# A fused attention and mixture kernel: the second mixture's opening rebuilt, its weight operands asked for sooner, one tile moved

## The chip, the cores and the metric

The kernel runs on one core of one Trainium2 chip. The metric is the device time of one execution in microseconds, as the median over executions. Engines are called PE (TensorE), DVE (VectorE), ACT (ScalarE), POOL (GpSimd) and SP (SyncE, which here only starts transfers). Each engine works through its own instructions in order, and semaphores join them.

## The reference

Three stages follow one another, all in float32:

- Attention over 4 batches, 8 heads, 576 positions, head size 64: features exp(±(x·w_phi − max|x·w_phi|)), 256 of them, on q and k; then `num = q' (k'ᵀ v)`, `den = q' · sum(k')`, `out = num / den`. It gives x with 2304 rows and 512 columns.
- A first mixture: softmax over rows and over slots of `x @ phi` (32 slots, 4 for each of 8 experts); the slots' inputs go through each expert's `relu(s @ w1) @ w2` and are mixed back to rows.
- A second mixture, by far the longest: `P = exp(x @ w_gate − max)`, normalised eight times over rows and columns in turn, and `out = sum over 8 experts e of P[:, e] * (relu(x @ w1[e]) @ w2[e])`, with w1 512×1024 and w2 1024×512.

## The kernel before

In the second mixture the 2304 rows are taken in 9 blocks of 256 rows for each of 8 experts, 72 blocks in all, expert after expert. Rows of x have rank 32 there (they are mixtures of 32 slots), so the first layer is a product of slot weights `ct` (a transposed tile for every 512 rows, `ct0` to `ct4`) with a stack `st` made once for each expert (`make_stack`, `spread_stack`, done inside the expert's predecessor's last block).

The second layer is written as seven half-size products, k = 0 to 6, in the form of Strassen and Winograd. For each block, `hidden` makes seven left operands from the first layer's results z: a11, a12 and a22 are the relu of quarters of z, and s1 to s4 are sums and differences of them. For float32 accuracy every operand is split into a rounded high part (ACT, tiles `hh_a`, `hh_s`) and the rest (`hl_a` by DVE, `hl_s` by POOL), and each product is 12 matmuls of 128×128 by 128×256. The right operands come from w2: b11, b21, b22 as they are, t1 to t4 as sums and differences (`w_sum` 0 to 3, each one POOL instruction), and `w_part` k makes the high part (ACT) and the rest (POOL) of the operand of product k. Operands live in a ring of ten buffers (`n = (7 * e + k) % NW`), so part k of one expert takes the buffer of product k−3 of the expert before.

`hidden` is a generator of five steps. In the main loop the steps for block i+1 run behind products 2 to 6 of block i, one step behind each product. After product 2 of a block, `first_layer` computes z of the next block into two PSUM tiles, each of which exists once. Behind each product, `take` adds its sum into the output rows `xo` (ACT or DVE for expert 0, DVE with the factor P for the others).

Two dictionaries say behind which block and product the operands of the next expert are asked for: `W_SUMS` and `W_PARTS`, keys (block, k); a key (9, k) means block 0 of the expert itself. POOL does these and the `hl_s` of `hidden` in program order.

`sinkhorn` is the generator of P: gate product, gate pass `plog` (18 small matmuls), maximum, exponential, then eight rounds of five steps each on DVE with one small matmul. Its rounds are threaded through the blocks of expert 0: `SINK = {1: 3, 5: 2}` asks for three steps behind product 1 and two behind product 5.

From the end of the attention on, every engine keeps the order of the program (`InOrder`), so its instructions all carry line 50 in the profile; one goes by the tile names. Blocks are counted from 0 here, and k counts products. The opening is what stands between the first mixture's end and the main loop:

```
sink = sinkhorn(); next(sink)
stacks = {0: make_stack(0)}
for k in (4, 5, 6): w_part(0, k)
spread_stack(stacks[0], 0)
next(sink); next(sink)
first_layer(0, 0); first_layer(0, 1)
next(sink)
for _ in hidden(0): pass
load_munits(4)
```

Of the kernel before, what the change touches and what calls it, by code (L numbers as in the profile page):

```python
# [17 lines left out]
NT = NTOK // 128  # L18
# [35 lines left out]
def tile_kernel(ctx: ExitStack, tc: tile.TileContext, a):  # L54
# [48 lines left out]
    def load_k(t):  # L103
        x = kp.tile([128, 512], F32, tag="kt", name=f"kt{t}")
        SP.dma_start(out=x, in_=a["kT"][t])
        kt_t[t] = x
# [292 lines left out]
    load_k(1)  # L399
    load_v(0)  # L400
    load_k(2)
    ident = load_const("ident", [128, 128])
    ones = load_const("ones", [128, 128])
    sel_e = load_const("sel_e", [128, 4], kp)
# [113 lines left out]
    mp = mp_cm.__enter__()  # L518

    ct = [const.tile([128, 512], F32R, tag=f"x{i}", name=f"ct{i}", bufs=1) for i in range(4)]  # L520
    ct.append(const.tile([128, 256], F32R, name="ct4", bufs=1))
    rep = [const.tile([128, 4, 128], F32R, tag=f"x{4 + i}", name=f"rep{i}", bufs=1) for i in range(2)]
    for i in range(2):
        G.dma_start(out=rep[i], in_=a["rep"][:, i * 512:(i + 1) * 512].rearrange("p (g c) -> p g c", g=4))
# [201 lines left out]
    def acc_tile(name):  # L726
        return pm.tile([128, 512], F32, tag="m", name=name)
# [30 lines left out]
    def sinkhorn():  # L758

        pg = acc_tile("pgate")  # L760
        for c in range(KC):
            PE.matmul(pg[:, 0:E], sot[:, c, :], wg[:, c, :], start=c == 0, stop=c == KC - 1)
        gst = cp.tile([128, E], F32R, name="gst")
        V.tensor_copy(out=gst, in_=pg[:, 0:E])
        V.tensor_tensor(out=gst[64:128, :], in0=pg[64:128, 0:E], in1=gst[64:128, :].bitcast(F32), op=ALU.subtract)
        yield
        pl = acc_tile("plog")
        for t in range(NT):
            PE.matmul(pl[:, t * E:(t + 1) * E], ct[t // 4][:, t % 4 * 128:(t % 4 + 1) * 128], gst, start=True, stop=True)
        yield  # L770
        Pf = P.rearrange("p t e -> p (t e)")
        V.tensor_copy(out=Pf, in_=pl[:, 0:NT * E])
        gm = cp.tile([128, 1], F32, name="gm")
        V.tensor_reduce(out=gm, in_=Pf, axis=AX.X, op=ALU.max)
        yield
        pg = acc_tile("pgm")
        PE.transpose(pg[0:1, 0:128], gm, ident)
        gm1 = cp.tile([1, 1], F32, name="gm1")
        V.tensor_reduce(out=gm1, in_=pg[0:1, 0:128], axis=AX.X, op=ALU.max)
        pg = acc_tile("pgb")  # L780
        PE.matmul(pg[:, 0:1], ones[0:1, :], gm1, start=True, stop=True)
        yield
        V.tensor_copy(out=gm, in_=pg[:, 0:1])
        V.tensor_scalar_sub(Pf, Pf, gm)
        A.activation(out=P, in_=P, func=AF.Exp)
        yield
        for it in range(8):
            rs = cp.tile([128, NT, 1], F32, tag="rs", name=f"rs{it}")
            V.tensor_reduce(out=rs, in_=P, axis=AX.X, op=ALU.add)
            V.tensor_scalar_add(rs, rs, 1e-9)  # L790
            V.reciprocal(out=rs, in_=rs)
            yield
            V.tensor_tensor(out=P, in0=P, in1=rs.to_broadcast([128, NT, E]), op=ALU.mult)
            yield
            cs = cp.tile([128, 1, E], F32, tag="cs", name=f"cs{it}")
            csf = cs.rearrange("p o e -> p (o e)")
            V.tensor_reduce(out=csf, in_=P.rearrange("p t e -> p e t"), axis=AX.X, op=ALU.add)
            yield
            pg = z_tile(0, f"pcs{it}")
            PE.matmul(pg[:, 0:E], ones, csf, start=True, stop=True)  # L800
            V.tensor_scalar(out=csf, in0=pg[:, 0:E], scalar1=1e-9, scalar2=float(E) / NTOK, op0=ALU.add, op1=ALU.mult)
            V.reciprocal(out=csf, in_=csf)
            yield
            V.tensor_tensor(out=P, in0=P, in1=cs.to_broadcast([128, NT, E]), op=ALU.mult)
            yield
# [12 lines left out]
    def hidden(i):  # L818

        z0, z1 = zs.pop((i, 0)), zs.pop((i, 1))  # L820
        z11, z21 = z0[:, :, 0:128], z0[:, :, 128:256]
        z12, z22 = z1[:, :, 0:128], z1[:, :, 128:256]

        def raw(name):
            return cp.tile([128, KH, 128], F32, tag="s", name=f"{name}_{i}", bufs=3)

        def hi_of(name, src, func):
            h = cp.tile([128, KH, 128], F32R, tag="hh", name=f"hh_{name}_{i}", bufs=7)
            A.activation(out=h, in_=src, func=func)
            l = cp.tile([128, KH, 128], F32R, tag="hl", name=f"hl_{name}_{i}", bufs=7)  # L830
            hop[i, name] = h, l

        def lo_z(name, z):
            h, l = hop[i, name]
            V.scalar_tensor_tensor(out=l, in0=z, scalar=0.0, in1=h.bitcast(F32), op0=ALU.max, op1=ALU.subtract)

        def lo_s(name, s):
            h, l = hop[i, name]
            G.tensor_tensor(out=l, in0=s, in1=h.bitcast(F32), op=ALU.subtract)

        def fused(name, z, s, op):
            o = raw(name)
            V.scalar_tensor_tensor(out=o, in0=z, scalar=0.0, in1=s, op0=ALU.max, op1=op)
            return o

        r22 = raw("r22")
        if i:
            A.activation(out=r22, in_=z22, func=AF.Relu)
            hi_of("a11", z11, AF.Relu)
        else:  # L850
            hi_of("a11", z11, AF.Relu)
            A.activation(out=r22, in_=z22, func=AF.Relu)
            lo_z("a11", z11)
        s1 = fused("s1", z21, r22, ALU.add)
        yield
        s2 = fused("s2", z11, s1, ALU.subtract)
        hi_of("a12", z12, AF.Relu)
        hi_of("s1", s1, AF.Copy)
        lo_s("s1", s1)
        if i:  # L860
            lo_z("a11", z11)
        yield
        r11 = raw("r11")
        hi_of("s2", s2, AF.Copy)
        A.activation(out=r11, in_=z11, func=AF.Relu)
        lo_s("s2", s2)
        lo_z("a12", z12)
        s4 = fused("s4", z12, s2, ALU.add)
        yield
        hi_of("a22", z22, AF.Relu)  # L870
        hi_of("s4", s4, AF.Copy)
        s3 = fused("s3", z21, r11, ALU.subtract)
        lo_s("s4", s4)
        yield
        hi_of("s3", s3, AF.Copy)
        lo_z("a22", z22)
        lo_s("s3", s3)
        yield
# [43 lines left out]
    sink = sinkhorn()  # L922
    next(sink)
    stacks = {0: make_stack(0)}
    for k in (4, 5, 6):
        w_part(0, k)
    spread_stack(stacks[0], 0)
# [2 lines left out]
    first_layer(0, 0)  # L930
    first_layer(0, 1)
    next(sink)
    for _ in hidden(0):
        pass
    load_munits(4)

    W_SUMS = {(3, 1): 0, (3, 6): 1, (5, 6): 2, (7, 6): 3}
    W_PARTS = {(2, 6): 0, (4, 6): 2, (6, 6): 1, (8, 1): 3, (8, 6): 4, (9, 0): 5, (9, 1): 6}
    SINK = {1: 3, 5: 2}
    making = iter(())  # L940
    for i, (e, blk) in enumerate(blocks):
        more = e + 1 < E
        if blk == 2 and more:
# [1 line left out]
        for k in range(7):  # L945
# [15 lines left out]
            if e and (blk + 9, k) in W_PARTS:  # L961
                w_part(e, W_PARTS[blk + 9, k])
            if e == 0:
                for _ in range(SINK.get(k, 0) - (blk == 0 and k == 1)):
                    next(sink, None)
            if i == NBLK - 1 and k in (3, 4):
                scale_row(k - 3)
# [68 lines left out]
```

## Time and profile before

| | |
|---|---|
| median of 3 runs | 1088.23 us (1085.76 to 1088.39) |
| profiled execution | 1086.3 us, of which the span from first to last instruction is 1084.1 us |
| mean granted TensorE clock | 0.995 |
| busy shares of the span | PE 97%, PE weight load 91%, DVE 68%, POOL 63%, ACT 53% |
| chain that ended last | PE 78%, POOL 11%, DVE 5%, issue 2%, DMA 2%, ACT 1% |
| second mixture | from about 271 us to the end |

The shares are means over stages with different limits. The chain followed back from the last instruction says which engine's work set the end at each point: where POOL stands in it, PE was waiting for POOL or for what POOL released. In the timeline views a line gives the start of a group of instructions, how long it lasted, engine, line, operation, output and inputs, how many, and in brackets how long the engine stood idle before it and what ended that.

### The profile page before, as it was taken

How to read it: one execution, taken by the hardware profiler on the slowest of the kernel's cores; microseconds unless marked ns; L12 is line 12 of the kernel's file. 1: busy time of each engine (PE TensorE's matmuls, PEld its weight loads, DVE VectorE, ACT ScalarE, POOL GpSimd, SP SyncE). 2: the span in 40 equal slices, each digit the busy share in tenths (PEclk: the TensorE clock that was granted, in tenths of full speed). 3: DMA queues.
4: the chain of work that ended last, by engine and by line, in shares of the span. 5: the costliest groups of instructions: out<-in, count | busy, mean ns of one | idle time of the engine just before them, and what ended most of it. 6: DMA issues, size and time to landing. Idle time of an engine off the chain costs nothing.

```text
span 1084.1 us, 23152 instructions
## 1 busy us (share of the span) xinstructions
PE 1052.2 (97%) x9206; PEld 982.0 (91%) x9206; DVE 732.0 (68%) x1518; ACT 569.8 (53%) x1009; POOL 687.3 (63%) x442
## 2 busy tenths in 40 slices
PE   7999999999899999999999999999999999999998
PEld 5688788853899999999999999999999999999998
DVE  6878777850578767665766666576667666665765
ACT  5665544312556576654556454655555564545542
POOL 4776551107556777777777577767777775777443
PEclk9999999999899999999999999999999999999999
DMA  7772115379400130022003100300220031000111
GB/s 264 246 272 88 54 40 205 146 279 399 158 2 2 36 121 1 2 79 79 2 1 117 40 2 16 141 2 1 79 79 1 2 112 46 2 1 21 54 45 60
DMA packets 22571, 89.26 MB, mean 82 GB/s; under 512 B 2752, under 2 KB 5568, under 8 KB 14272
## 3 DMA queue, kind: packets, MB, share of 16 engines
q1 hardware_dynamic: 22176, 87.26, 22.2%
q8 instruction: 73, 1.20, 0.5%
q0 software_dynamic: 288, 0.52, 0.2%
q14 instruction: 34, 0.28, 0.1%
HBM read 83.05 MB, written 4.72 MB: 81 GB/s over the span
## 4 chain that ended last, share of the span: by engine, by line
PE 78%; POOL 11%; DVE 5%; issue 2%; DMA 2%; ACT 1%; SPq 0%; POOLq 0%; DVEq 0%; ACTq 0%
PE x L50 30%; PE y L50 14%; PE z L50 12%; PE num L271 6%; POOL hl_s L50 5%; POOL w_t L50 3%; PE kvacc L179 3%; POOL w_b L50 2%; PE ut L246 1%; PE ps L50 1%; DVE s L50 1%; PE kvp L218 1%; DMA moe_w<-in_moe_w 1%; PE pk L142 1%; PE ph L50 1%
## 5 line engine op out<-in xcount | busy, mean ns | idle before, releaser
L50 POOL TENSOR_TENSOR hl_s<-s,hh_s 128x512 fp32r<-128x512 f32 x288 | 367.5, 1298 | 230.1 <-ACT hh_s L50 214.0
L50 PE MATMUL x<-w_t,hh_s 128*128 128x256 f32 x1152 | 205.4, 278 | 3.9 <-DVE xo L50 2.7
L50 ACT ACTIVATE hh_s<-s 128x512 fp32r<-128x512 f32 x288 | 175.7, 629 | 53.0 <-DVE s L50 49.1
L50 PEld LDWEIGHTS x<-w_t,hh_s 128*128 128x128 f32 x1152 | 173.8, 188 | 5.3 <-issue 3.9
L50 DVE SCALAR_TENSOR_TENSOR xo<-x,P,xo 128x256 f32<-128x256 f32 x252 | 121.1, 481 | 75.3 <-PE x L50 75.3
L50 ACT ACTIVATE hh_a<-z 128x512 fp32r<-128x512 f32 x216 | 122.2, 600 | 90.1 <-DVE s L50 88.3
L50 ACT ACTIVATE r<-z 128x512 f32<-128x512 f32 x144 | 86.1, 598 | 156.6 <-PE z L50 156.2
L50 PE MATMUL x<-w_t,hl_s 128*128 128x256 f32 x576 | 159.7, 277 | 0.0
L50 DVE SCALAR_TENSOR_TENSOR s<-z,r 128x512 f32<-128x512 f32 x144 | 98.9, 687 | 86.7 <-ACT hh_a L50 82.2
L50 DVE SCALAR_TENSOR_TENSOR hl_a<-z,hh_a 128x512 fp32r<-128x512 f32 x216 | 147.4, 683 | 0.0
L50 DVE SCALAR_TENSOR_TENSOR s<-z,s 128x512 f32<-128x512 f32 x144 | 98.5, 684 | 19.4 <-POOL hl_s L50 17.9
L50 PE MATMUL x<-w_t,hh_a 128*128 128x256 f32 x576 | 104.2, 279 | 6.3 <-POOL w_t L50 4.9
L50 PEld LDWEIGHTS x<-w_t,hl_s 128*128 128x128 f32 x576 | 108.3, 188 | 0.0
L50 PE MATMUL y<-w_b,hh_s 128*128 128x256 f32 x576 | 103.8, 278 | 0.2 <-POOL w_b L50 0.2
L50 PE MATMUL x<-w_b,hh_a 128*128 128x256 f32 x576 | 103.1, 279 | 0.0
L50 PE MATMUL z<-w_b,hh_a 128*128 128x256 f32 x576 | 103.0, 279 | 0.0
L50 PE MATMUL y<-w_t,hh_s 128*128 128x256 f32 x576 | 102.9, 278 | 0.0
L50 PEld LDWEIGHTS x<-w_t,hh_a 128*128 128x128 f32 x576 | 87.5, 188 | 7.9 <-POOL w_t L50 6.2
L50 PEld LDWEIGHTS z<-w_b,hh_a 128*128 128x128 f32 x576 | 87.3, 189 | 2.9 <-issue 2.9
L50 PEld LDWEIGHTS y<-w_b,hh_s 128*128 128x128 f32 x576 | 87.5, 188 | 1.4 <-POOL w_b L50 1.3
L50 PEld LDWEIGHTS x<-w_b,hh_a 128*128 128x128 f32 x576 | 87.7, 190 | 0.0
L50 PEld LDWEIGHTS y<-w_t,hh_s 128*128 128x128 f32 x576 | 87.6, 188 | 0.0
(213 smaller groups left out, 2342.1 us busy)
## 6 DMA issues: line engine op xcount, KB each, us to landing
moe_w<-in_moe_w SPq DMA_DIRECT2D x64, 1024.0 KB, 6.9
vt<-in_vb SPq DMA_DIRECT2D x20, 256.0 KB, 3.7
kt<-in_kT SPq DMA_DIRECT2D x18, 256.0 KB, 3.1
qt<-in_qT SPq DMA_DIRECT2D x18, 256.0 KB, 2.8
out<-xo SPq DMA_DIRECT2D x18, 128.0 KB, 1.7
out<-xo SPq DMA_DIRECT2D x9, 256.0 KB, 2.0
rep<-in_rep POOLq DMA_DIRECT2D x2, 256.0 KB, 5.8
bd<-in_bd SPq DMA_DIRECT2D x1, 384.0 KB, 4.3
```

The source lines that it names most:

```text
L50: return lambda *args, **kwargs: self.tc.keep_in_program_order(make(*args, **kwargs))
L142: PE.matmul(o, hi[:, s], wbdh, start=True, stop=False)
L179: PE.matmul(acc[64 * j:64 * j + 64, p * 256:(p + 1) * 256], v[:, (2 * p + j) * D:(2 * p + j + 1) * D], phik[:, 2 * p + j].rearrange("p c f ...
L218: PE.matmul(ps[:, c * 192:(c + 1) * 192], kvt[:, p * 256 + c * 128:p * 256 + (c + 1) * 128], bd[:, p], start=True, stop=True)
L246: PE.transpose(ps[:, j * 128:(j + 1) * 128], uq_t[t][hh][:, j * 128:(j + 1) * 128], ident)
L271: PE.matmul(ps[r0:r1, j * XW:(j + 1) * XW], phiq[:, c, j * 128 + r0:j * 128 + r1], kvs_t[b][:, c, 4 * hh + j, :], start=c == 0, stop=c == 1,)
```

## The change

```
@@ attention's loads
     load_k(2)
+    ct4 = const.tile([128, 256], F32R, name="ct4", bufs=1)
     ident = load_const("ident", [128, 128])
@@ first mixture
-    ct.append(const.tile([128, 256], F32R, name="ct4", bufs=1))
+    ct.append(ct4)
@@ sinkhorn
         for t in range(NT):
             PE.matmul(pl[:, t * E:(t + 1) * E], ct[t // 4][...], gst, start=True, stop=True)
+            if t == NT // 2 - 1:
+                yield
         yield
@@
         V.tensor_reduce(out=gm1, in_=pg[0:1, 0:128], axis=AX.X, op=ALU.max)
+        yield
         pg = acc_tile("pgb")
@@ hidden
         hi_of("a12", z12, AF.Relu)
-        hi_of("s1", s1, AF.Copy)
-        lo_s("s1", s1)
         if i:
+            hi_of("s1", s1, AF.Copy)
+            lo_s("s1", s1)
             lo_z("a11", z11)
         yield
         r11 = raw("r11")
         hi_of("s2", s2, AF.Copy)
+        if i == 0:
+            hi_of("s1", s1, AF.Copy)
         A.activation(out=r11, in_=z11, func=AF.Relu)
         lo_s("s2", s2)
+        if i == 0:
+            lo_s("s1", s1)
         lo_z("a12", z12)
@@ the opening
     stacks = {0: make_stack(0)}
+    next(sink)
     for k in (4, 5, 6):
         w_part(0, k)
@@
-    for _ in hidden(0):
-        pass
+    making = hidden(0)
+    for _ in range(3):
+        next(making)
     load_munits(4)

-    W_SUMS = {(3, 1): 0, (3, 6): 1, (5, 6): 2, (7, 6): 3}
-    W_PARTS = {(2, 6): 0, (4, 6): 2, (6, 6): 1, (8, 1): 3, (8, 6): 4, (9, 0): 5, (9, 1): 6}
+    W_SUMS = {(3, 1): 0, (3, 6): 1, (5, 6): 2, (7, 1): 3}
+    W_PARTS = {(2, 6): 0, (4, 6): 2, (6, 6): 1, (8, 0): 3, (8, 1): 4, (8, 6): 5, (9, 0): 6}
     SINK = {1: 3, 5: 2}
-    making = iter(())
+    next_after = {(0, 0): 1}
@@ main loop
             if e == 0:
-                for _ in range(SINK.get(k, 0) - (blk == 0 and k == 1)):
+                for _ in range(next_after.get((blk, k), 0) + SINK.get(k, 0) - (blk == 0 and k == 1)):
                     next(sink, None)
```

In words. The tile `ct4` is allotted among the first constants instead of among the later ones. The gate pass is issued in two halves of 9 matmuls: the first between `make_stack` and `spread_stack`, the second where the whole stood. The broadcast of the maximum (`pgb`) moves from in front of block 0's products to behind product 0. For block 0 only three of the five steps of `hidden` come ahead of the loop, with the halves of s2 made before those of s1; the fourth and fifth step come behind products 0 and 1. For every next expert, sum 3 moves from behind product 6 to behind product 1 of block 7, part 3 from product 1 to product 0 of block 8, part 4 from product 6 to product 1 of block 8, part 5 from product 0 of the expert's own block 0 to product 6 of block 8, and part 6 from product 1 to product 0 of the expert's own block 0.

## Rows read from the trace of the kernel before

**Rows 1.** The list of waits (engine, line, waited for: us in total, times, longest).

```profile
PE x L50 <- POOL w_t L50: 4.9, 7, 0.7
```

**Rows 2.** PE timeline: first layers (start us, us), first handover, last handover.

```profile
391.25 1.11 PE L50 MATMUL z<-ct,st 128*128 128x256 f32 x8
...
403.56 1.11 PE L50 MATMUL z<-ct,st 128*128 128x256 f32 x8
...
978.23 1.11 PE L50 MATMUL z<-ct,st 128*128 128x256 f32 x8
...
988.71 1.10 PE L50 MATMUL z<-ct,st 128*128 128x256 f32 x8
...
1001.18 1.11 PE L50 MATMUL z<-ct,st 128*128 128x256 f32 x8
```

**Rows 3.** PE timeline: products late at the first handover.

```profile
394.93 0.53 PE L50 MATMUL y<-w_b,hh_s 128*128 128x256 f32 x2
...
397.42 0.39 PE L50 MATMUL x<-w_t,hh_a 128*128 128x256 f32 x1 [0.71 <-POOL w_t L50]
...
402.11 0.47 PE L50 MATMUL x<-w_t,hh_s 128*128 128x256 f32 x2 [0.45 <-DVE xo L50]
```

**Rows 4.** POOL timeline: experts 0 and 1, block 7 to the handover.

```profile
365.37 2.39 POOL L50 TENSOR_TENSOR w_b<-moe_w,w_b 128x1024 fp32r<-128x1024 f32 x1
...
376.20 2.39 POOL L50 TENSOR_TENSOR moe_w<-moe_w,t 128x1024 f32<-128x1024 f32 x1
...
380.54 2.40 POOL L50 TENSOR_TENSOR w_t<-moe_w,w_t 128x1024 fp32r<-128x1024 f32 x1 [1.95 <-ACT w_t L50]
...
390.25 2.41 POOL L50 TENSOR_TENSOR w_t<-moe_w,w_t 128x1024 fp32r<-128x1024 f32 x1
...
392.61 2.41 POOL L50 TENSOR_TENSOR w_b<-moe_w,w_b 128x1024 fp32r<-128x1024 f32 x1
...
394.98 2.39 POOL L50 TENSOR_TENSOR w_t<-moe_w,w_t 128x1024 fp32r<-128x1024 f32 x1
...
397.32 2.54 POOL L50 TENSOR_TENSOR hl_s<-s,hh_s 128x512 fp32r<-128x512 f32 x2
```

**Rows 5.** POOL timeline: expert 1, block 7.

```profile
469.81 2.54 POOL L50 TENSOR_TENSOR hl_s<-s,hh_s 128x512 fp32r<-128x512 f32 x2 [1.85 <-ACT hh_s L50]
```

**Rows 6.** DVE timeline: a take while POOL makes a part.

```profile
391.45 0.48 DVE L50 SCALAR_TENSOR_TENSOR xo<-x,P,xo 128x256 f32<-128x256 f32 x1 [0.88 <-PE x L50]
```

**Rows 7.** POOL timeline: expert 0, block 3, sum 0.

```profile
323.12 2.40 POOL L50 TENSOR_TENSOR moe_w<-moe_w 128x1024 f32<-128x1024 f32 x1
```

**Rows 8.** DVE timeline: expert 0, rounds on P, block 3 and block 7.

```profile
320.95 2.25 DVE L50 TENSOR_TENSOR P<-P,cs 128x144 f32<-128x144 f32 x1
...
323.58 1.97 DVE L50 TENSOR_SCALAR rs<-rs 128x18 f32<-128x18 f32 x1
...
368.30 0.18 DVE L50 TENSOR_SCALAR rs<-rs 128x18 f32<-128x18 f32 x1
```

**Rows 9.** PE timeline: expert 0, block 3, product 6.

```profile
328.18 0.50 PE L50 MATMUL x<-w_t,hh_a 128*128 128x256 f32 x2 [1.42 <-DVE xo L50]
```

**Rows 10.** PE timeline: the opening.

```profile
277.06 1.19 PE L50 MATMUL pr<-st,rep 128*128 128x256 f32 x8 [1.06 <-issue]
...
287.78 0.39 PE L50 MATMUL x<-w_t,hh_s 128*128 128x256 f32 x1 [1.16 <-ACT xo L50]
...
289.27 1.11 PE L50 MATMUL z<-ct,st 128*128 128x256 f32 x8
```

**Rows 11.** DVE timeline: the opening, s4 and the rest of a22.

```profile
284.87 0.69 DVE L50 SCALAR_TENSOR_TENSOR s<-z,s 128x512 f32<-128x512 f32 x1 [0.73 <-POOL hl_s L50]
...
286.72 0.68 DVE L50 SCALAR_TENSOR_TENSOR hl_a<-z,hh_a 128x512 fp32r<-128x512 f32 x1
```

**Rows 12.** Stretches (us; busy PE, PEld, DVE, ACT, POOL; clock; DMA): opening's low clock.

```profile
282.80:283.60 0.80, 0.80 (x6) 0.80 (x5) 0.77 (x3) 0.66 (x2) 0.04 (x1) 0.50 0.98 358
...
284.40:285.20 0.80, 0.80 (x5) 0.80 (x5) 0.33 (x1) 0.29 (x1) 0.80 (x2) 0.50 0.99 399
```

More of the change, by code (lines that the diff above doesn't have):

```diff
@@ L401, in tile_kernel @@
     load_k(2)
+    ct4 = const.tile([128, 256], F32R, name="ct4", bufs=1)
     ident = load_const("ident", [128, 128])
@@ L520, in tile_kernel @@
     ct = [const.tile([128, 512], F32R, tag=f"x{i}", name=f"ct{i}", bufs=1) for i in range(4)]
-    ct.append(const.tile([128, 256], F32R, name="ct4", bufs=1))
+    ct.append(ct4)
     rep = [const.tile([128, 4, 128], F32R, tag=f"x{4 + i}", name=f"rep{i}", bufs=1) for i in range(2)]
@@ L769, in sinkhorn @@
             PE.matmul(pl[:, t * E:(t + 1) * E], ct[t // 4][:, t % 4 * 128:(t % 4 + 1) * 128], gst, start=True, stop=True)
+            if t == NT // 2 - 1:
+                yield
         yield
@@ L779, in sinkhorn @@
         V.tensor_reduce(out=gm1, in_=pg[0:1, 0:128], axis=AX.X, op=ALU.max)
+        yield
         pg = acc_tile("pgb")
@@ L857, in hidden @@
         hi_of("a12", z12, AF.Relu)
-        hi_of("s1", s1, AF.Copy)
-        lo_s("s1", s1)
         if i:
+            hi_of("s1", s1, AF.Copy)
+            lo_s("s1", s1)
             lo_z("a11", z11)
@@ L864, in hidden @@
         hi_of("s2", s2, AF.Copy)
+        if i == 0:
+            hi_of("s1", s1, AF.Copy)
         A.activation(out=r11, in_=z11, func=AF.Relu)
         lo_s("s2", s2)
+        if i == 0:
+            lo_s("s1", s1)
         lo_z("a12", z12)
@@ L924, in tile_kernel @@
     stacks = {0: make_stack(0)}
+    next(sink)
     for k in (4, 5, 6):
@@ L932, in tile_kernel @@
     next(sink)
-    for _ in hidden(0):
-        pass
+    making = hidden(0)
+    for _ in range(3):
+        next(making)
     load_munits(4)
-    W_SUMS = {(3, 1): 0, (3, 6): 1, (5, 6): 2, (7, 6): 3}
-    W_PARTS = {(2, 6): 0, (4, 6): 2, (6, 6): 1, (8, 1): 3, (8, 6): 4, (9, 0): 5, (9, 1): 6}
+    W_SUMS = {(3, 1): 0, (3, 6): 1, (5, 6): 2, (7, 1): 3}
+    W_PARTS = {(2, 6): 0, (4, 6): 2, (6, 6): 1, (8, 0): 3, (8, 1): 4, (8, 6): 5, (9, 0): 6}
     SINK = {1: 3, 5: 2}
-    making = iter(())
+    next_after = {(0, 0): 1}
     for i, (e, blk) in enumerate(blocks):
@@ L963, in tile_kernel @@
             if e == 0:
-                for _ in range(SINK.get(k, 0) - (blk == 0 and k == 1)):
+                for _ in range(next_after.get((blk, k), 0) + SINK.get(k, 0) - (blk == 0 and k == 1)):
                     next(sink, None)
```

## The prediction

> **What bounds the kernel now.** I read the page's busy shares and its chain of waits first, then the list of waits, then the timelines of PE, POOL, ACT and DVE around each place that the change touches. The reader is to see that PE is the bound nearly everywhere in the second mixture, so only PE's idle time and its low clock can be won there. The first layers mark the blocks: from 978.23 to 988.71 us one block takes 10.48 us, and at that pace PE has no gaps [rows 2]. The list of waits names one thing that holds PE seven times, a part of the right operands made by POOL: 4.9 us in all [rows 1]. Seven is the number of handovers from one expert to the next. Each handover costs more than that entry shows: between the first layers on its two sides lie 391.25 to 403.56, or 12.31 us, at the first, and 988.71 to 1001.18, or 12.47 us, at the last [rows 2]. The losses over 10.48 us are 1.83 and 1.99 us; added over the seven handovers they are 13.9 us.
>
> Why the first handover loses its 1.83 us is seen in three PE lines: product 5 starts with a pair that lasts 0.53 us, product 6 waits 0.71 us for POOL, and product 2 of the next block waits 0.45 us for DVE's take [rows 3]. POOL's lines show one cause for all three. From 390.25 to 397.37 us POOL makes parts 4, 5 and 6 in one piece, and only then the two subtractions for s1 and s2 [rows 4]. Part 5 ends at 395.02 and part 6 at 397.37 us, just when PE needs them. The subtractions come late too, so DVE, which needs a buffer that the first of them frees, runs its takes late.
>
> **The change part by part.**
>
> *Parts 3 to 6 asked for sooner.* No instruction is added; four POOL and four ACT instructions move for each of seven experts. POOL's order becomes: part 3 in the time after 376.2, part 4 where part 3 stood (380.54), part 5 where part 4 stood (390.25), part 6 where part 5 stood (392.61 to 395.02) [rows 4]. Part 3 finds POOL free because sum 3, which ran at 376.20, leaves that place. Part 5 is then ready 2.27 us before product 5's line at 394.93, part 6 about 1.3 us before product 6 would start, and the subtractions start at about 395.0 instead of 397.32. They would like to start some 0.3 us before that, at the pace of other blocks; DVE stands idle 0.88 us between takes [rows 6], so this is covered. The ring doesn't hold the parts back: part k needs the product k−3 of the expert before, and each is asked for behind that product. The gain is therefore up to 13.9 us; if the backlog only moved it would be 0. I take 13.9, as POOL's free times before 380.54 (1.95 us idle even with sum 3 there [rows 4]) hold one more instruction of 2.4 us. If that cover were gone, each handover would keep its 1.8 to 2.0 us.
>
> *Sum 3 behind product 1 of block 7.* Seven POOL instructions of 2.39 us move ahead of that block's subtractions. In experts 1 to 6 POOL stands idle 1.85 us there [rows 5], so the subtractions come 0.5 us late; DVE's 0.88 us between takes [rows 6] cover it: nothing, with 7 × 0.5 = 3.5 us as the far end. In expert 0 it is not nothing. There POOL makes part 1 at 365.37 [rows 4] and sum 3 would follow at once, until about 370.1, while DVE does the rounds on P. Block 3 has just that sequence now, a part and then a sum at 323.12 [rows 7]: DVE's product on P lasts 2.25 us and ends with POOL's part, the addition on `rs` lasts 1.97 us and ends with POOL's sum, where the same addition takes 0.18 us in block 7 [rows 8]. PE then waits 1.42 us for DVE at product 6 [rows 9]. I charge block 7 of expert 0 the same, 1.4 us; between 0 and 2.4 us, the whole of sum 3.
>
> Here a page bears on the case. The Trainium skill, "SBUF — State Buffer", section "SBUF: two separate sides", says that VectorE and GpSimd share one pair of ports as an exclusive lock for a whole instruction, when VectorE's has two inputs in SBUF or runs in a two-port mode; the loser waits. Rows 8 agree for the operations on P, and by that rule the 1.4 us must be paid; were bandwidth merely shared, the sum below would be 1.4 us better. The same rule leaves alone an operation that reads PSUM, and the take of 0.48 us beside a part of POOL [rows 6] agrees.
>
> *The opening.* Before, PE waits 1.06 us ahead of `spread_stack` for DVE's stack and 1.16 us ahead of product 2 for the take of product 0, which stands on ACT behind all of `hidden` [rows 10]; and the clock is at 0.50, the level of 1.2 GHz, in the three stretches of 0.8 us from 282.8 to 285.2 us, under products 0 and 1 (the first and the last in [rows 12]). Nine matmuls of the gate pass now fill the 1.06 us, so z, and all that follows, comes about 1.0 us sooner. With two steps of `hidden` behind products, the take gets its place early and product 2 starts without its wait. But the two subtractions on POOL change places: s4, which waits for the one of s1 and starts at 284.87 now [rows 11], waits for the second of the pair instead: 1.0 sooner and, with POOL's second subtraction ahead (1.27 us, half of the pair in [rows 5]) and ACT's hi part of s2 starting behind s2 instead of s1 (0.7), 2.0 later, so at about 285.9. Behind it on DVE come s3, the take of product 1 and the rest of a22. That last one is at 286.72 now [rows 11] and would be at about 287.45, ending at 288.1. The next first layer overwrites the tile that it reads, and so can't start before 288.2; it starts at 289.27 now [rows 10]. The gain is 1.1 us at that point, and PE stands idle in front of it for 1 to 2 us. Two things can take it back: the subtraction on P, waiting for POOL's last two subtractions as in rows 8, makes the next block's `hidden` late; and idle PE time could bring the low clock back a few us later, as the sparse stretch ahead of 282.8 did. Bounds: at best all of 1.06 + 1.16 and half of the 2.4 us at low clock, 3.4 us gained; at worst POOL's 1.27 and a low stretch of its own, 1.2, so 2.5 us lost. I take 0.4 us gained, the 1.1 less what a chance of about a half of either loss is worth. The broadcast `pgb` behind product 0 costs nothing: its result is wanted only behind product 1.
>
> *`ct4` moved, SP and POOL's other queues.* The tile keeps its size and nothing else lies in its place: 0, and neither engine nor queue waits more. The four loads of the opening (SP) issue nothing new and no transfer is moved past them; part 6's earlier end lets the next loads start about 2 us sooner, and nothing waits for those in the list of waits: 0.
>
> The sum is −13.9 + 1.4 − 0.4 = −12.9 us. Made against the profiled execution's 1086.3 us (span 1084.1 and 2.2 us around it), it gives 1073.4; against the median of the runs, 1088.23, it gives 1075.3. I say **1075 us**. By itself this case reaches from 1071 (opening at its best) to 1079 (opening at its worst, 0.4 us late in each block 7).
>
> **The rivals.**
>
> *Half of the handover stays.* Parts 5 and 6 come in time but the subtractions still come late enough that product 2 waits for the take. For it: part 6 still stands in front of them and ends at about 395.0, a little after they could start. Against: DVE's 0.88 us idle. It would save 0.14 + 0.71 us of the first handover's lines [rows 3], about 6 us in seven; with the other terms, 6.0 − 1.4 + 0.4 = 5.0 us: about 1083.
>
> *The parts come no sooner.* The program asks sooner, but ACT's casts stand in order behind others and behind the product that frees the buffer, so POOL runs the same train. For it: at 380.54 POOL's wait ended with ACT's cast, which stands behind the stack's casts [rows 4]. Against: part 3 now stands ahead of those. Then only the 1.4 us and the opening remain: about 1089, within what counts as no change.
>
> *Slower: POOL's moved instructions hold DVE everywhere.* The rule of rows 8 would hold for DVE's reads of PSUM as well. Sum 3 would cost what block 3 pays, 1.42 us [rows 9], in all seven blocks 7, and part 3, which now runs while DVE casts the stack in block 8, would put `spread_stack` back by up to 2.4 − 0.5 = 1.9 us. Seven times 3.3 is 23.2 us, less 13.9: 9.3 us slower, about 1097. It decides from 2.0 us for each expert. Against it: rows 6.
>
> **How the numbers follow.** The forecast gets 0.74, half a handover 0.14, no sooner 0.07, slower 0.05. The range of 8 in 10 runs from 1070 to 1083, from a little under the forecast's own lower end to the half handover. A measurement of this kernel tells from no change what is over about 0.3%, 3.3 us. The first two cases are faster but for a small part: 0.87. The third is no change, with a little of the second: 0.07. The rest, 0.06, is slower.
>
> **What would show it.** In the profile after: the list of waits has no line of PE waiting for `w_t` from POOL seven times; the first layers at the handovers are 10.5 us apart; POOL's two subtractions follow part 6 at about the time of rows 4's 394.98, shifted by what was won before. In block 7 of expert 0 the addition on `rs` lasts about 2 us and product 6 has a new wait of some 1.4 us for DVE's take. In the opening the wait of 1.06 us is gone, the first layer of block 1 waits for DVE, and a second low stretch of the clock either comes behind it or doesn't. Wrong would be handovers of over 11 us, or blocks 7 of experts 1 to 6 longer than now.

## The result, and the profile after

The changed kernel takes 1071.2 us, the median of 4 runs (1068.3 to 1076.1), against 1087.1 us for the kernel before in the same series (1085.8 to 1088.4). The ratio is 0.986 [0.982, 0.990], so some 15 us are gone (11 to 20). The forecast was 1075 us.

The profiled execution after has a span of 1066.3 us, 17.8 us less than before. The list of waits of TensorE is read first (the tile that PE was to write, the engine and tile that it waited for; total us, times, longest us). The rows left out here are the attention's, and some of under 1 us:

```profile
...
PE x L50 <- DVE xo L50: 2.8, 2, 1.4
...
PE z L50 <- DVE gm L50: 2.3, 1, 2.3
...
```

The entry that stood seven times before, PE waiting for `w_t` from POOL [rows 1], is gone. The largest that are left in the second mixture are two waits for `xo`, 1.4 us each, of which the one in block 3 of expert 0 stood there before [rows 9], and one for `gm`, 2.3 us. The first layers stand so (PE timeline of after, around the first handover and the last):

```profile
378.39 1.11 PE L50 MATMUL z<-ct,st 128*128 128x256 f32 x8
...
388.87 1.11 PE L50 MATMUL z<-ct,st 128*128 128x256 f32 x8
...
399.35 1.11 PE L50 MATMUL z<-ct,st 128*128 128x256 f32 x8
...
973.43 1.11 PE L50 MATMUL z<-ct,st 128*128 128x256 f32 x8
...
983.91 1.11 PE L50 MATMUL z<-ct,st 128*128 128x256 f32 x8
```

Both handovers, 388.87 to 399.35 and 973.43 to 983.91, now take 10.48 us, where 12.31 and 12.47 stood [rows 2]; so do the five between them. POOL shows why (its timeline of after, where rows 4 showed the train):

```profile
373.99 2.39 POOL L50 TENSOR_TENSOR w_t<-moe_w,w_t 128x1024 fp32r<-128x1024 f32 x1
378.16 2.40 POOL L50 TENSOR_TENSOR w_t<-moe_w,w_t 128x1024 fp32r<-128x1024 f32 x1 [1.77 <-ACT w_t L50]
...
387.87 2.41 POOL L50 TENSOR_TENSOR w_b<-moe_w,w_b 128x1024 fp32r<-128x1024 f32 x1
390.23 2.41 POOL L50 TENSOR_TENSOR w_t<-moe_w,w_t 128x1024 fp32r<-128x1024 f32 x1
392.60 2.55 POOL L50 TENSOR_TENSOR hl_s<-s,hh_s 128x512 fp32r<-128x512 f32 x2
```

Parts 3 and 4 now stand at 373.99 and 378.16. At the end of the preparation POOL makes two parts (5 and 6) in one piece, not three, and the subtractions follow at 3.7 us behind the first layer at 388.87; before, they came 6.1 us behind theirs (397.32 against 391.25, [rows 2, 4]).

The whole difference of the two profiled executions adds up over four stretches of PE's timeline. "z" is the first first layer of the second mixture, at 280.00 before and 275.67 after.

| stretch | before, us | after, us | difference |
|---|---|---|---|
| start to the gate's first product | 271.46 | 269.75 | −1.71 |
| gate's first product to z | 8.54 | 5.92 | −2.62 |
| z to the end of the last matmul | 800.73 | 787.22 | −13.51 |
| behind the last matmul | 3.37 | 3.37 | 0.00 |

The first row and 1.6 us of the second are not the change's: before, the granted clock was 0.57 from 159 to 163 us and 0.50 (1.2 GHz) from 272 to 275 us, after it was 1.00 in these places. The run times, which have such stretches on either side, show 2 us less than the profiles do.

The third row is the change. The seven handovers give 13.88 us. The interval that ends expert 0 (first layer of block 8 to the next one, with the late products of block 7 and the next stack in it) grew from 14.44 to 15.91 us, 1.47 us. The opening from z to the first layer of block 2 grew from 20.03 to 20.56, 0.53 us. A part that I had not forecast falls on the same interval of the other experts, 13.74 to 13.54 us, six times 0.20, and on the last block, 16.67 to 16.10. That is −13.88 + 1.47 + 0.53 − 1.20 − 0.57 = −13.65, against −13.51; most of what is missing is one interval of expert 6, 10.57 us before and 10.76 after.

### The profile page after: what moved, and what is told of

Same layout as the page of the kernel before. It is cut to its first block, busy times and chain, and to the rows that moved or that the text cites. A ratio compares the mean times of both kernels' runs of the same rounds, so it can differ in the third digit from the quotient of the medians.

```text
span 1066.3 us, 23151 instructions
## 1 busy us (share of the span) xinstructions
PE 1039.9 (98%) x9206; PEld 974.1 (91%) x9206; DVE 734.3 (69%) x1518; ACT 571.5 (54%) x1009; POOL 688.3 (65%) x442
## 4 chain that ended last, share of the span: by engine, by line
PE 90%; DVE 4%; POOL 2%; issue 2%; DMA 2%; ACT 1%; SPq 0%; DVEq 0%; POOLq 0%; ACTq 0%
PE x L50 36%; PE y L50 18%; PE z L50 15%; PE num L271 6%; PE kvacc L179 2%; PE ut L246 1%; PE ps L50 1%; PE kvp L218 1%; DMA moe_w<-in_moe_w 1%; PE ph L50 1%; PE pk L142 1%; PE pk L144 1%; POOL zs L197 1%; PE pq L142 1%; PE pq L144 1%
## 5 line engine op out<-in xcount | busy, mean ns | idle before, releaser
L50 PE MATMUL x<-w_t,hh_a 128*128 128x256 f32 x576 | 101.9, 277 | 2.8 <-DVE xo L50 2.8
L50 PE MATMUL y<-w_b,hh_s 128*128 128x256 f32 x576 | 101.5, 276 | 0.0
```

The lines of the kernel that those rows point to most:

```text
L50: return lambda *args, **kwargs: self.tc.keep_in_program_order(make(*args, **kwargs))
```

## The experiments

"Block n's interval" is the time from the first layer that computes z of block n to the next one; the handovers are block 1's intervals of experts 1 to 7. The kernel before was run beside each of them; its median was 1086.4 us for the first eight, 1087.6 us for the last four. A difference in us is the ratio's distance from 1 times that median.

**The handover dictionaries alone.** The kernel before, with

```
-    W_SUMS = {(3, 1): 0, (3, 6): 1, (5, 6): 2, (7, 6): 3}
-    W_PARTS = {(2, 6): 0, (4, 6): 2, (6, 6): 1, (8, 1): 3, (8, 6): 4, (9, 0): 5, (9, 1): 6}
+    W_SUMS = {(3, 1): 0, (3, 6): 1, (5, 6): 2, (7, 1): 3}
+    W_PARTS = {(2, 6): 0, (4, 6): 2, (6, 6): 1, (8, 0): 3, (8, 1): 4, (8, 6): 5, (9, 0): 6}
```

> The kernel before with the two dictionaries alone changed (sum 3, parts 3 to 6 asked for sooner), opening and ct4 as before. Theory (POOL's train of parts at the handover is the loss): the first layers at all seven handovers are 10.5 us apart instead of 12.3 to 12.6, block 7 of expert 0 is 1.4 us longer, and the time is 12.5 us below before. Rival (the opening, or ct4's place, carries much of the change's gain): the time is under 8 us below before. Rival (parts come no sooner): 0 to 1.4 us slower.

Measured: 1076.0 us, ratio 0.989 [0.988, 0.991], 11.5 us less (9.6 to 13.4). All seven handovers take 10.48 us, and in expert 0 PE waits once more for the take behind DVE's rounds (PE timeline):

```profile
372.60 0.50 PE L50 MATMUL x<-w_t,hh_a 128*128 128x256 f32 x2 [1.25 <-DVE xo L50]
```

Its interval from z to the end of the last matmul is 788.31 us, 12.42 less than before: 13.88 less 1.47. So the handover is the dictionaries' alone, and most of the gain; the rival of under 8 us is out.

**Everything but the dictionaries.** The kernel after with the two lines of before.

> The changed kernel with the two dictionaries as before: only opening and ct4 are new. Theory: handovers 12.3 to 12.6 us apart as before; block 0's first layer about 1 us sooner after the gate product than before at equal clock, block 1's first layer waits some 2.2 us for DVE, and by block 2's first layer 0.4 us are left: the time is 0 to 0.5 us below before, plus or minus what low stretches of the clock make. Rival (opening worth 4 us, the 4.2 us by which block 1's first layer is earlier in the profile after): 3 to 4 us below before in every pair of profiles with the same mean clock.

Measured: 1084.7 us, ratio 0.999 [0.997, 1.000], 1.4 us less (0 to 2.8). The handovers are back at 12.3 to 12.6 us; the interval of block 8 stays at 13.54 us. The rival's 3 to 4 us are out. The two experiments make up the change: 11.5 and 1.4 us are 12.9, inside the 11 to 20 of the whole.

**Sum 3 back behind product 6.** The kernel after, with

```
-    W_SUMS = {(3, 1): 0, (3, 6): 1, (5, 6): 2, (7, 1): 3}
+    W_SUMS = {(3, 1): 0, (3, 6): 1, (5, 6): 2, (7, 6): 3}
```

> The changed kernel with sum 3 behind product 6 of block 7 again, parts 3 to 6 as changed. Theory (POOL's two instructions in one piece beside the rounds on P cost 1.4 us in block 7 of expert 0, and POOL has room before the handover): block 7 of expert 0 back to its 14.4 us between first layers, handovers still 10.5 us; 1.4 us below the changed kernel. Rival (part 3 needs the place of sum 3, so the train at the handover comes back): handovers of 11 to 12.5 us, 4 to 12 us slower than the changed kernel.

Measured: 1070.8 us, ratio 0.985 [0.983, 0.987]. The last interval of expert 0 is 14.24 us (365.92 to 380.16), where after has 15.91: the step costs 1.67 us, and the wait of 1.39 us in it is gone. The seven handovers stay at 10.48 us, so sum 3's move was not needed for them. The time is only 0.4 us under that of after, within the scatter of either. The profiled execution shows what runs of this kernel differ by: a stretch at half clock right where the prediction feared one (busy time by engine of three stretches, then the granted clock):

```profile
283.80:287.80 4.00, 1.76 (x15) 1.59 (x14) 3.08 (x6) 1.63 (x3) 2.05 (x3) 1.00 0.56 233
288.00:291.60 3.60, 3.60 (x21) 3.60 (x20) 2.94 (x6) 1.82 (x6) 1.01 (x1) 0.55 0.02 5
292.00:296.00 4.00, 4.00 (x37) 4.00 (x37) 2.74 (x6) 2.81 (x7) 2.55 (x2) 1.00 0.00 0
```

PE is busy 1.76 of the 4 us around its wait for the first layer of block 1 (at 287.14), and behind that the clock is at 0.55 with PE busy throughout. Block 1's interval is then 12.44 us in place of 11.15.

**One GpSimd step a block.** The kernel after, with

```
-    W_SUMS = {(3, 1): 0, (3, 6): 1, (5, 6): 2, (7, 1): 3}
-    W_PARTS = {(2, 6): 0, (4, 6): 2, (6, 6): 1, (8, 0): 3, (8, 1): 4, (8, 6): 5, (9, 0): 6}
+    W_SUMS = {(2, 6): 0, (3, 6): 1, (5, 6): 2, (7, 6): 3}
+    W_PARTS = {(1, 6): 0, (4, 6): 2, (6, 6): 1, (8, 0): 3, (8, 1): 4, (8, 6): 5, (9, 0): 6}
-        if blk == 2 and more:
+        if blk == 1 and more:
```

> The changed kernel with one sum or part behind product 6 of each of the blocks 1 to 7 (part 0, sum 0, sum 1, part 2, sum 2, part 1, sum 3) and parts 3 to 6 as changed, so that no two POOL instructions on weights stand in one piece beside the rounds on P. Theory (the lock on the port holds DVE's addition on rs until the second of two): blocks 3 and 7 of expert 0 lose no time, first layers there 10.8 and 14.4 us apart instead of 12.4 and 15.9; 3.1 us below the changed kernel. Rival (the wait at product 6 of these blocks comes from something else in those blocks): no change in block 3.

Measured: 1067.9 us, ratio 0.982 [0.980, 0.984]. With no sum behind a part in blocks 3 and 7 of expert 0, PE's two waits for `xo` are gone. The wait in block 3 stands at its product 6, which lies behind the first layer of block 4: block 4's interval is 10.76 us (before and after: 12.45 and 12.44), and the one that ends expert 0 is 14.25 us (15.91 in after).

```profile
319.65 1.11 PE L50 MATMUL z<-ct,st 128*128 128x256 f32 x8
...
330.41 1.11 PE L50 MATMUL z<-ct,st 128*128 128x256 f32 x8
...
362.70 1.12 PE L50 MATMUL z<-ct,st 128*128 128x256 f32 x8
...
376.95 1.11 PE L50 MATMUL z<-ct,st 128*128 128x256 f32 x8
```

That is 1.7 us in each of the two places, and the median lies 3.3 us under that of after. In block 7 DVE's product on P still lasts 2.24 us beside POOL's one instruction; what is gone is the second hold, on the addition to `rs`, which lasts 0.18 us there.

**Parts 5 and 6 asked for late again.** The kernel after, with

```
-    W_PARTS = {..., (8, 6): 5, (9, 0): 6}
+    W_PARTS = {..., (9, 0): 5, (9, 1): 6}
```

> The kernel after, with VectorE's parts 5 and 6 of a preparation asked for at blocks (9,0) and (9,1) again, as before; parts 3 and 4 and sum 3 stay sooner. Theory (GpSimd's backlog sets the arrival of a part: in the trace of before its quads of the preparation stand at 390.25, 392.61, 394.98 and 397.32 back to back, so it takes parts 5 and 6 only when 3 and 4 are through): with 3 and 4 sooner, GpSimd is free by (9,0) and reaches the last two before TensorE wants them; handovers stay at 10.48 us, time within 2 us of the kernel after (about 1071). Rival (the asking time of the last two parts is what made TensorE wait): the first layer waits for w_t again at 4 to 5 us in sum over a few handovers, handovers at 11.5 to 12.4 us, time 1078 to 1085.

Measured: 1072.4 us, ratio 0.987 [0.985, 0.989], that of after. The handovers are 10.48 us and POOL takes the two parts back to back as before (its timeline):

```profile
393.70 2.41 POOL L50 TENSOR_TENSOR w_b<-moe_w,w_b 128x1024 fp32r<-128x1024 f32 x1
396.05 2.43 POOL L50 TENSOR_TENSOR w_t<-moe_w,w_t 128x1024 fp32r<-128x1024 f32 x1
```

(The expectation calls the parts VectorE's; they are GpSimd's.) This execution came to block 2 late: its clock stood at half from 270 to 290 us. Counted from its first layer of block 2, at 302.04, they start 91.66 and 94.01 us on; in after, from 296.23, it is 91.64 and 94.00. The asking of the last two parts sets nothing: POOL reaches them at the same time anyway. What decides is that parts 3 and 4 come sooner, so that one part less stands in front of the subtractions: part 4, asked for behind product 1 of block 8 instead of product 6, left the train. Parts 3 and 4 were not tried one by one.

**The gate in two halves, alone.** The kernel before, with

```
+            if t == NT // 2 - 1:
+                yield
...
+    next(sink)
```

> The kernel before with one part alone: the gate's pass in two halves; the feature steps, ct4 and the dictionaries as before. Theory: the idle 1.06 us that TensorE has ahead of its reduction product in the opening goes, pgate to z takes 5.9 us and not 6.9 at full clock, and the first layer of block 1 comes as much sooner: 1.0 us below before. Rival (the gate is not on the path, a VectorE step of block 0's features is): pgate to z falls but the first layer of block 1 stands where it stood, 0 us. Handovers stay at 12.3 to 12.6 us in both.

Measured: 1085.9 us, ratio 1.000 [0.998, 1.001]: −0.4 us, from −2.0 to +1.1, which holds both answers. In the trace, the first half of the gate stands where PE idled 1.06 us ahead of `pr` [rows 10], and no idle time is left there (PE timeline):

```profile
277.05 1.24 PE L50 MATMUL plog<-gst,ct 128*128 128x8 f32 x9
278.16 1.18 PE L50 MATMUL pr<-st,rep 128*128 128x256 f32 x8
279.18 1.06 PE L50 MATMUL plog<-gst,ct 128*128 128x8 f32 x9
```

From the gate's first product to z it is 7.47 us, 1.5 of them because 32 matmuls of `ps` took 3.4 us at half clock, 1.93 at full clock elsewhere. That leaves 5.97, as expected. Whether the next step comes as much sooner is read at product 2, which waits for the take on ACT (PE timeline of this kernel, then of "the handover dictionaries alone", which has the old opening):

```profile
287.88 0.79 PE L50 MATMUL x<-w_t,hh_s 128*128 128x256 f32 x2 [2.19 <-ACT xo L50]
```

```profile
287.43 0.50 PE L50 MATMUL x<-w_t,hh_s 128*128 128x256 f32 x2 [1.23 <-ACT xo L50]
```

Product 2 starts 15.24 us behind the gate's first product here, 13.74 without the 1.5, and 14.69 there: the 1.0 us is still won. It starts 7.78 us behind z in both, though products 0 and 1 ran at full clock here and at half clock there (281 to 285 us): in the old opening a low clock at that place costs nothing, the wait for the take covers it. Here the half-clock stretch came later, from 287.3 to 290.6, under product 2, and took back what had been won; the first layer of block 1 itself is therefore not seen to come sooner in this trace.

**The order of the feature steps, alone.** The kernel before with `making = hidden(0)`, three steps of it ahead of the loop, the halves of s2 ahead of those of s1, and `pgb` behind product 0.

> The kernel before with one part alone: block 0's feature steps moved among the products of the opening, its gate in one pass and all else as before. Theory: the order of these steps costs a little, z to the first layer of block 2 takes 20.5 us in place of 20.0 at full clock, 0.5 us above before. Rival (the order is what shortens the opening, the halves only follow it): the first layer of block 1 comes 0.5 us or more sooner than in before, time 0.5 us below. Handovers as before in both.

Measured: 1086.1 us, ratio 0.999 [0.998, 1.001], −0.9 us, from −2.2 to +0.5. z to the first layer of block 2 is 21.19 us, but the clock stood at half from 277 to 286 us, so the 0.5 us can't be read. The time reaches the theory's 0.5 above only at its end and holds the rival's 0.5 below. Inconclusive: the price of the order is known only from the kernels with both parts (20.56 against 20.03).

**`ct4` alone.** The kernel before, with

```
+    ct4 = const.tile([128, 256], F32R, name="ct4", bufs=1)
...
-    ct.append(const.tile([128, 256], F32R, name="ct4", bufs=1))
+    ct.append(ct4)
```

> The kernel before with one part alone: ct4's place, which the program gives at 16512 bytes of a partition in place of 32032. Theory (the matmuls that read ct4 at 32032, 32 past a multiple of 64, set a slower pace behind them): the seven stretches with 0.353 us per three matmuls, at 467.4 to 474.1 in the trace of before the first of those I count, go to 0.340, block 8's interval falls from 13.74 to 13.54 us in each expert, and the time by about 2 us. Rival (the rebuilt opening changed the pace, not ct4): 13.74 and 0.353 stay, time within 0.5 us of before.

Measured: 1084.8 us, ratio 0.999 [0.997, 1.000], 1.5 us less (0 to 3.0). The stretches of slower products behind the first layers that read `ct4` are gone. In the timeline of before, right behind the first layer that begins block 8's interval of expert 1 (466.44), one group of three products follows the next at 0.353 us:

```profile
467.39 0.40 PE L50 MATMUL y<-w_t,hh_s 128*128 128x256 f32 x2
...
467.75 0.40 PE L50 MATMUL y<-w_t,hh_s 128*128 128x256 f32 x2
...
468.10 0.40 PE L50 MATMUL y<-w_t,hh_s 128*128 128x256 f32 x2
```

With `ct4` moved, the same products follow at 0.340 us:

```profile
464.84 0.39 PE L50 MATMUL y<-w_t,hh_s 128*128 128x256 f32 x2
...
465.18 0.39 PE L50 MATMUL y<-w_t,hh_s 128*128 128x256 f32 x2
```

Block 8's interval is 13.54 us in every later expert, the last block 16.10, and z to the end of the last matmul 1.70 us less than before. No instruction changed in this kernel, so the rebuilt opening is not the cause. What moved with `ct4` are the other constants, `ct0` to `ct3` among them, by 1024 bytes; the slow stretches of before follow the first layers that read `ct4` and not those that read `ct0` to `ct3`. The slower pace is not `ct4`'s alone, though. It also comes where PE had been held up: in before behind the waits for POOL at the handovers of experts 2, 4 and 6 (from 497 to 503 us the first time), in after through block 1 of the opening, behind a wait of 2.25 us, and from 923 to 928 us, where one group of three came 0.08 us late. In these places it ended with a first layer.

**`ct4` at another place, twice.** First the kernel before with a small constant ahead of it padded, so that `ct4` begins 32 bytes further; then the kernel after with `ct4` itself 32 bytes further.

```
-        rd = const.tile([128, 4, 1], F32, name="rd_held") if held else ...
+        rd = const.tile([128, 16, 1], F32, name="rd_held")[:, 0:4] if held else ...
```

> The kernel before with one part alone: a small constant ahead of ct4 is padded by 32 bytes, so that ct4 is still made where before makes it but begins at 32064 bytes of a partition (a multiple of 64) in place of 32032. Theory (the offset of 32 within 64 bytes sets the slow pace of the products behind it): the seven stretches at 0.353 us per three matmuls are gone, block 8's interval is 13.54 us in each expert, time about 2 us below before (1084 to 1085). Rival (another property of the old place): they stay, block 8 at 13.74, time as before.

```
-    ct4 = const.tile([128, 256], F32R, name="ct4", bufs=1)
+    ct4 = const.tile([128, 272], F32R, name="ct4", bufs=1)[:, 8:264]
```

> The kernel after with ct4 shifted by 32 bytes, to 16544 bytes of a partition, and all else as after. Theory (the offset of 32 within 64 bytes sets the slow pace): the seven stretches come back, block 8 at 13.74 us in each expert, about 2 us above the kernel after (1073). Rival (the place in the partition, not the offset): block 8 stays at 13.54 and the time at that of the kernel after.

Measured: 1105.9 us, ratio 1.017 [1.015, 1.019], and 1107.3 us, ratio 1.018 [1.017, 1.020], which is 36 us above after. Neither answer was expected. The padding had shifted more than `ct4`. In the built programs all tiles of the right operands (`w0_...`, `w1_...`) begin 32 bytes further in the first and 64 bytes further in the second, and so do the pools beside them, while the features `hh` and `hl` and the stack `st` keep their places. In each of the matmuls the 128×128 tile that PE's weight load takes is one of `hh`, `hl` or `st` (the stationary operand); the 128×256 tile that is streamed past it is a right operand or `ct` (the moving operand). So the moving operands were shifted and the stationary ones were not. Every block of the second mixture that has no wait is longer, those of expert 7 too, in which nothing is prepared for a next expert any more. First layers in the first kernel (10.89 us apart), then in the second (11.02 us), where both before and after have 10.48:

```profile
621.74 1.11 PE L50 MATMUL z<-ct,st 128*128 128x256 f32 x8
...
632.63 1.11 PE L50 MATMUL z<-ct,st 128*128 128x256 f32 x8
```

```profile
621.33 1.10 PE L50 MATMUL z<-ct,st 128*128 128x256 f32 x8
...
632.35 1.10 PE L50 MATMUL z<-ct,st 128*128 128x256 f32 x8
```

No wait stands between them: PE is busy throughout (22.00 of 22 us, at granted clock 1.00, in the first kernel):

```profile
610.00:632.00 22.00, 22.00 (x188) 22.00 (x187) 14.84 (x28) 11.02 (x19) 11.22 (x10) 1.00 0.00 1
```

The first kernel's blocks are 3.9% longer (10.89 / 10.48), the second's 5.2% (11.02 / 10.48). Offsets within 64 bytes don't explain it as a rule: the right operands went from an offset of 32 to one of 0 in the first kernel and kept 32 in the second, and both got slower. For `ct4` by itself the two kernels decide little, as the products are slower everywhere: its block 8 takes 3.0 us more than the other blocks in both, where before has 3.26 and after 3.06, so no stretch of its own is seen in either, not even with `ct4` back at an offset of 32. What stays is that the place of the moving operands alone, with the same instructions, changes the pace. Which property of the place does it is open.

**A version better than both.** The kernel of "one GpSimd step a block", with `ct4` moved and the gate in halves, but with block 0's feature steps ahead of its products as in the kernel before.

> The kernel of the run e4_one_a_block (one GpSimd step a block for sums and parts), with ct4 moved and the gate in two halves, but block 0's feature steps all ahead of the products as in the kernel before. Theory (the halves give 1.0 us, the new order of the steps takes 0.5 us back): z to the first layer of block 2 at 20.0 us in place of 20.5 at full clock, block 1 to block 2 at 10.8 us and not 11.15, time 0.5 us below the run e4_one_a_block, about 1067.4. Rival (the order of the steps is worth something of its own): 0.5 us or more above it, about 1068.5.

Measured: 1067.2 us (1065.4 to 1071.9), ratio 0.981 [0.979, 0.983]; with "one GpSimd step a block" at 0.982 [0.980, 0.984], the two can't be told apart. Block 1's interval is 10.76 us, as expected; z to block 2 is 20.99, with the clock at half from 271 to 288 us, so the 20.0 can't be read. The medians of both lie 3 to 4 us under that of the kernel after, while the intervals of the ratios overlap a little with its own; the traces show the 3.3 us of the two waits gone in both.

**The clock alone.** The kernel of "everything but the dictionaries", once more.

> A second profile of the kernel of the run e2_opening (the kernel after with the dictionaries of before), for the clock alone. Theory (where the half-clock stretches of the opening fall differs from one execution to the next, by tenths of the clock's mean and 1 to 3 us of the time, and no edit sets it): the handovers stay at 12.3 to 12.6 us and block 8 at 13.54, while the half-clock stretches between 20 and 300 us stand elsewhere than in the first profile. Rival (they belong to the kernel): the same stretches again.

Measured: 1086.9 us in this one run, 3.9 us over the 1083.0 of the first profiled one. The first had one half-clock stretch ahead of its last microseconds, at 159 to 163 us. The second had four, around 23, 161, 275 and 292 us. Its rows for the last two (busy time by engine, then clock) and those of the first in the same places:

```profile
274.00:278.00 4.00, 4.00 (x38) 2.04 (x37) 0.79 (x4) 1.39 (x2) 4.00 (x2) 0.57 0.31 74
291.00:295.00 4.00, 4.00 (x24) 4.00 (x23) 3.02 (x6) 2.91 (x8) 1.01 (x2) 0.57 0.01 4
```

```profile
274.00:278.00 4.00, 4.00 (x47) 3.40 (x37) 0.85 (x2) 1.39 (x3) 4.00 (x3) 1.00 0.72 240
291.00:295.00 4.00, 4.00 (x36) 4.00 (x36) 3.74 (x9) 2.96 (x7) 2.81 (x3) 1.00 0.00 0
```

In the stretch from 291 us PE issues 24 matmuls in 4 us or 36, from the same kernel. So a half-clock stretch in one profile and not in another doesn't show the effect of an edit.

## Why the prediction was right

**The handovers: right, 13.9 forecast, 13.88 found.** The step said that one cause, POOL's train of three parts, stood behind the three late products. With the train cut, all three went at once; half a handover (the rival at 1083) did not stay, and the dictionaries alone give the whole of it. Two details of the step were not needed. It let all four parts come sooner, but with parts 5 and 6 asked for as before the handovers stay at 10.48 us: the sooner parts 3 and 4 decide. And it made room for part 3 by moving sum 3, but with sum 3 back the handovers stay at 10.48 us too.

**Sum 3 in block 7: right, 1.4 forecast, 1.67 found in expert 0, nothing in the others.** DVE's timeline of after shows the product on P and the addition on `rs`, and POOL's below it the part and the sum beside them:

```profile
361.87 2.25 DVE L50 TENSOR_TENSOR P<-P,cs 128x144 f32<-128x144 f32 x1
364.15 0.30 DVE L50 TENSOR_REDUCE rs<-P 128x18 f32<-128x144 f32 x1
364.49 1.97 DVE L50 TENSOR_SCALAR rs<-rs 128x18 f32<-128x18 f32 x1
```

```profile
361.56 2.39 POOL L50 TENSOR_TENSOR w_b<-moe_w,w_b 128x1024 fp32r<-128x1024 f32 x1
364.03 2.39 POOL L50 TENSOR_TENSOR moe_w<-moe_w,t 128x1024 f32<-128x1024 f32 x1
```

The product on P ends at 364.12 and POOL's part at 363.95; the addition on `rs`, 0.18 us before [rows 8], lasts 1.97 and ends at 366.46, POOL's sum at 366.42. PE pays at product 6:

```profile
369.08 0.50 PE L50 MATMUL x<-w_t,hh_a 128*128 128x256 f32 x2 [1.39 <-DVE xo L50]
```

The rule of the Trainium skill, "SBUF — State Buffer", section "SBUF: two separate sides", that the pair of ports is locked for a whole instruction, is borne out by these ends; the reduction (0.30) between them was not held. The slower rival, the same hold for reads of PSUM in every block 7, would have made the blocks 7 of experts 1 to 6 longer; with the dictionaries alone they are as they were, 10.48 us for block 7's interval and 13.74 for block 8's.

**The opening: 0.4 forecast, 0.45 found in two profiles; the steps up to block 1's first layer right, the size in part luck.** From the gate's first product to the first layer of block 2 it is 26.93 us with the old opening ("the handover dictionaries alone", whose low clock under products 0 and 1 is covered) and 26.48 in after. Up to the first layer of block 1 the steps were as worked out (PE, then DVE, timelines of after):

```profile
272.61 1.17 PE L50 MATMUL plog<-gst,ct 128*128 128x8 f32 x9
273.73 1.18 PE L50 MATMUL pr<-st,rep 128*128 128x256 f32 x8
...
285.08 1.20 PE L50 MATMUL z<-ct,st 128*128 128x256 f32 x8 [2.25 <-DVE gm L50]
```

```profile
282.52 0.69 DVE L50 SCALAR_TENSOR_TENSOR s<-z,s 128x512 f32<-128x512 f32 x1 [2.72 <-POOL hl_s L50]
```

The halves fill the idle 1.06 us; s4 then waits 2.72 us for the second subtraction on POOL, where it waited 0.73 before [rows 11], and starts 1.98 us later behind z, of which 2.0 were forecast; and PE idles 2.25 us ahead of block 1's first layer, of which 1 to 2 were forecast. The profile puts that wait down to `gm`, a copy that ends 0.07 us behind the rest of a22, which the forecast had named; both stand at the end of the same piece of DVE's work. The first layer of block 1 comes 0.85 us sooner behind the gate, of 1.1 forecast.

The 0.4 us was not the worth of one course of things but the 1.1 less a chance of either of two losses, and in after neither loss came. No product of block 1 waits for its features, and the clock stays at 1.00. What took 0.39 us back (block 1's interval is 11.15 us, 10.76 with the old opening) was a loss that the forecast did not have: behind the wait all products of block 1 follow at the slower pace, 0.353 us for three matmuls in place of 0.340, which is 0.35 us over its 26 groups of three (first the PE timeline of after, then of before, in the same place):

```profile
286.11 0.40 PE L50 MATMUL y<-w_t,hh_s 128*128 128x256 f32 x2
...
286.46 0.40 PE L50 MATMUL y<-w_t,hh_s 128*128 128x256 f32 x2
...
286.82 0.40 PE L50 MATMUL y<-w_t,hh_s 128*128 128x256 f32 x2
```

```profile
290.57 0.39 PE L50 MATMUL y<-w_t,hh_s 128*128 128x256 f32 x2
...
290.91 0.39 PE L50 MATMUL y<-w_t,hh_s 128*128 128x256 f32 x2
...
291.25 0.39 PE L50 MATMUL y<-w_t,hh_s 128*128 128x256 f32 x2
```

The feared low clock behind the idle time did come in other executions: the new opening has 11.15 us for block 1 in after and in the first profile of "everything but the dictionaries", and 12.42 to 12.66, with a half-clock stretch, in three others. With it the new opening is some 0.8 us slower than the old one. So over several executions the opening looks worth about nothing, and the times don't speak against it: "everything but the dictionaries", which holds the opening and `ct4`, is 1.4 us under before, and `ct4` alone 1.5, each give or take 1.5. The forecast's best case was also too high by its 1.2 us for the low clock under products 0 and 1, which cost nothing there.

**`ct4`: wrong, 0 forecast.** The step "the tile keeps its size and nothing else lies in its place: 0" held for queues and transfers, and missed that the place of an operand that the products read can set their pace. Nor did nothing else move: the other constants went 1024 bytes further. It measured 1.5 us (0 to 3.0) by the times and 2.0 by the intervals (7 × 0.20 + 0.57). With it the terms, as measured in profiles without low clock where it counts, are −13.88 + 1.67 − 0.45 − 1.97 = −14.6 us, against 15.3 (11 to 20) from the ratio.

So the forecast of 12.9 was short by 1.7 us by the traces: the one term that had been put at nothing gave 2.0 more, and sum 3 cost 0.3 more than forecast. Against the 1087.1 us that the kernel before took in this series the forecast's sum gives 1074.2 us; the times alone, with 11 to 20 us, can't tell 12.9 from 14.6.

## What to carry to other kernels

Where several products run late at one place, look on the engine that feeds them for one train of instructions, and cut the train where one of its members can run in idle time of a block earlier; here asking sooner for the last two members of the train brought nothing. A part and a sum of GpSimd back to back beside VectorE's work on SBUF tiles cost TensorE 1.7 us here, and spreading them, one step a block, gives that back. Before a few microseconds are credited to an edit, look whether the moved tiles shifted others, and whether half-clock stretches fell into the same places in both profiles.

## What was not expected of the hardware

The place of the moving operands in a partition, by 32 or 64 bytes and with all instructions the same, changed the pace of products that wait for nothing by 3.9 to 5.2% (a block of 10.48 us became 10.89 or 11.02); these kernels took 18 us more than before and 36 us more than after. In the kernels before and after most blocks keep the faster pace, 0.340 us for three matmuls. The slower one, 0.353, shows in before for 6.7 us at a time behind the first layers that read `ct4`, through the last block, and behind three of the handovers' waits, and in after behind the opening's wait and once more, from 923 to 928 us; it ended with the next first layer. Padding of other shifts, to find the rule of it, was not tried.
